# Two attention blocks on one core: V's load on SyncE's queue in a fixed order, and the remainder transposes of steps 4 to 125 by DMA

## The chip, the core and the metric

The kernel runs on one core of a Trainium2 chip. The core has TensorE (PE, which multiplies matrices), VectorE (DVE), ScalarE (ACT), GpSimd (POOL) and SyncE (SP), each with its own stream of instructions. Data moves between the device memory and the on-chip memory by DMA; SP and ACT each issue DMAs into a queue of their own (q1 and q10 in the profile), and 16 DMA engines serve both. The metric is device time in microseconds (us). The kernel before takes 772.24 us, the median of 3 runs (771.94 to 772.95).

## The reference

Two independent problems A and B of the same shape stand side by side in the output. For each, with x of 16x80x576, K and V caches of 16x16x512x128, wq of 576x4096 and wo of 4096x576, all bf16:

```python
q = (x @ wq).reshape(B, Sq, Hq, Dh).transpose(0, 2, 1, 3)      # Hq = 32 heads, Dh = 128
k = jnp.repeat(k_cache, 2, axis=1); v = jnp.repeat(v_cache, 2, axis=1)
scores = jnp.einsum("bhqd,bhkd->bhqk", q, k) * (Dh ** -0.5)
p = softmax(scores, axis=-1)
o = jnp.einsum("bhqk,bhkd->bhqd", p, v)
return o.transpose(0, 2, 1, 3).reshape(B, Sq, Hq * Dh) @ wo
```

Two query heads share one head of K and V, so each K/V head has 160 query rows and 512 keys. The output is 16x80x1152: A's 576 columns, then B's.

## The kernel before, in words

**Steps.** The work is cut into 128 steps (units, U), 64 for each problem. A step is one batch element and four K/V heads. It loads K of the four heads with one transposing DMA (`em_ldk`, L744 to L746, 512 KB) and V with one plain DMA (`em_ldv`, L748 to L750, 512 KB). Each K/V head has 160 query rows and PE's tile has 128, so a step has five score tiles of 128x512: one for the first 128 rows of each head (k = 1 to 4), and one, the **remainder** (k = 0), that holds the last 32 rows of all four heads.

**One score tile.** PE multiplies Q by K into a PSUM bank (`em_qk` L796, the remainder `em_qkr` L782), DVE takes the negated row maximum (`em_max` L805), ACT the exponential with the row sum (`em_exp` L809), DVE the reciprocal (`em_rcp` L815), POOL normalises the tile (`em_nrm` L818). The tile then has to be transposed to pT. By default PE does it with four 128x128 transposes (`em_tr` L824) and DVE copies the result out of PSUM (`em_ptev` L832, the remainder's L830). For the remainders of the steps that `RSEL` (L67) names, SP issues one transposing DMA from p_sb to pT instead (`em_rtr` L836), and there is neither a PE transpose nor a DVE copy. In those steps the remainder also has a reciprocal of its own (`RG`, L66). Then PE multiplies pT by V (`em_pv` L870), 16 matmuls in a step, and ACT takes the result to oT (`em_oev` L886).

**Beside the steps** PE computes Q from x and wq (L672, evicted by ACT L683 or DVE L684) and the output product with wo (L923, evicted at L935, L944 and L951), whose results are stored by SP (L957). Weights come in pieces through SP's queue: wq (L647, L650), wo (L712), and problem B's x by transposing DMAs (L615).

**What sets the order.** A planner inside the kernel's own code (`_Sched`) simulates all engines with assumed durations and writes out, for each engine, a fixed list of instructions; semaphores between them are worked out from that order. Each operation has a stream, a duration, and for the loads a `grid`: a step and an offset from that step's planned time (`tv` plus an offset in us) before which it is not placed. `ahead` lifts its priority above other operations that are ready. Buffers: five slots for K (`NK`), four for V (`NV`), three for pT (`NPT`). K of step U is placed at the time of step U - 6 (`KLEAD`) plus `GK`, V at U - 2 (`VLEAD`) plus `GV`, a remainder's DMA at U - 2 (`RLEAD`) plus `GR_`, a weight piece at its own step (`cycle`, L597 to L606, at most one piece in a step) plus `GW`. A step's scores run 13 tiles (`LA`), 2.6 steps, ahead of its products. From step 10 on K also waits for the PE instruction that the plan has finished just before it (`hard`, L369 to L372). `_Dma.issue` (L120 to L144) is the planner's model of the two queues: when a transfer's data moves, and how long the issuing engine is held. In it a transposing DMA (kind T) of SP and a copy of V (kind V) on ACT's queue wait for each other (`lock`, `copy`).

**Before the change** V of steps 4 to 127 is issued by ACT (`VENG`, L54; 124 loads; the first four are SP's). The remainders of 78 of the 128 steps go by DMA: steps 24 to 45, 70 to 75 and 94 to 125 all, in 18 to 23, 46 to 49, 62 to 69 and 76 to 93 the odd ones, and none before 18 and from 50 to 61.

Of the kernel before, what the change touches and what calls it, by code (L numbers as in the profile page):

```python
# [23 lines left out]
VLAT = 1.05  # L24
VGEN = 2.75
CLAT = 1.3
KLEAD = 6
GK = -1.0
VLEAD = 2
GV = -3.4  # L30
RLEAD = 2
GR_ = 0.95
GW = -3.7
QL0 = 15.0
QL1 = 11.0
KC = 1.85
# [14 lines left out]
NWC = 4  # L51
BANKS = dict(S=(0, 1, 2, 6), T=(3, 4), O=(5, 7), M=(7, 5), M0=(7, 5, 6, 3, 4), M1=(7, 6), ML=(7, 5, 6, 0, 1))
NML = 12
VENG = "act"  # L54
VDUR = 0.42
VU0 = 14
KU0 = 10
XM = dict(wo=6.0, wq=6.0, wqb=6.0, RT=1.5, V=1.5, K=2.0, x=3.0)
# [5 lines left out]
WOC = 1.05  # L64
XDMA = True
RG = (((0, 1, 2, 3, 4),), ((0,), (1, 2, 3, 4)))  # L66
RSEL = ((18, 24, (1, 3)), (24, 46, (0, 1, 2, 3)), (46, 50, (1, 3)), (62, 70, (1, 3)), (70, 76, (0, 1, 2, 3)), (76, 94, (1, 3)), (94, 126, (0, 1, 2, 3)))  # L67
RDC = 0.5
RDK = 2.0
RDO = 10.0  # L70
# [42 lines left out]
class _Dma:  # L113
# [6 lines left out]
    def issue(self, e, st, op):  # L120
        ring = self.ring
        if op.kind == "T":
            d0 = max(st + TLAT, ring["sp"])
            if self.copy[0] < d0 + op.cost and self.copy[1] > d0:
                d0 = self.copy[1]
            end = max(d0 + op.cost, st + op.dur + 0.3)
            self.lock = (d0, end)
            ring["sp"] = end
            return end, max(st + op.dur, end - QRING)
        if op.kind == "V":  # L130
            d0 = max(st + VLAT, ring["act"])
            if self.lock[0] <= d0 < self.lock[1]:
                d0 = self.lock[1]
            end = max(d0 + op.cost, st + VLAT + VGEN)
            self.copy = (d0, end)
            ring["act"] = end
            return end, st + op.dur
        d0 = max(st + CLAT, ring[e])
        c = op.cost
        if e == "sp" and self.copy[0] < d0 + c and self.copy[1] > d0:  # L140
            c += min(c, self.copy[1] - d0)
        end = d0 + c
        ring[e] = end
        return end, max(st + op.dur, end - 6.0)  # L144
# [277 lines left out]
def bass_concat_heads__gqa_block_cached__gqa_block_cached__near_ridge_kernel(  # L422
# [27 lines left out]
    with ExitStack() as es:  # L450
# [21 lines left out]

        sem_names = (["e_pe", "e_act", "e_dve", "e_pool", "d_x00", "d_x01", "d_x10", "d_x11", "d_wo0", "d_wo1",
                      "d_wq0", "d_wq1", "d_wqs", "d_wqt"]
                     + ["d_out%d" % i for i in range(NOSB)]
                     + ["d_r%d" % i for i in range(NPT)]
                     + ["d_k%d" % i for i in range(NK)] + ["d_v%d" % i for i in range(NV)])
# [4 lines left out]
        def R(res, ver):  # L482
            return (res, ver)
# [58 lines left out]
        for half in range(NPP):  # L542
            x_ap = probs[0][0]
            for part, (k0, k1) in enumerate(XP):
                def em_ldx(e, x_ap=x_ap, half=half, k0=k0, k1=k1):
# [5 lines left out]
                      writes=[R(("xs", half * NRT + k_), 0) for k_ in range(k0, k1)], dsem="d_x%d%d" % (half, part),  # L551
# [46 lines left out]
        n = 3  # L598
# [9 lines left out]
        for half in range(NPP):  # L608
            x_ap = probs[1][0]
            st0 = UPR + 16 * half - lead[NG // 2 + 2 * half]  # L610
            for ck in range(5):
                def em_ldxt(e, x_ap=x_ap, half=half, ck=ck):
                    src = x_ap.rearrange("b s d -> (b s) d")[half * NROW:(half + 1) * NROW, :]
                    c0 = ck * 128 if ck < 4 else D - 128
                    return e.dma_start_transpose(xT[:, half, ck:ck + 1, :],  # L615
                                                 src[:, c0:c0 + 128].rearrange("n (c d) -> n c d", c=1))

                S.add("sp", 5.0 * cycle[("x", half, ck)] - 4.0, em_ldxt,
                      writes=[R(("xT", half, b_), 1) for b_ in range(NRT)] if ck == 0 else [R(("xT", half, "t", ck), 1)],
                      dsem="d_x%d0" % half, name="ldxt%d.%d" % (half, ck), stream="x", dur=1.3, cost=0.62, kind="T",  # L620
                      grid=(cycle[("x", half, ck)], GW))

        def qpos(goct, bl):
            return (2 * goct + bl // 4) % NQB * 4 + bl % 4
# [2 lines left out]
        for goct in range(NG):  # L627
# [6 lines left out]
            for pi, (c0, c1) in enumerate(pieces):  # L634
# [9 lines left out]
                for j, (k0, k1, n0, n1) in enumerate(parts):  # L644
                    def em_ldw(e, wq_ap=wq_ap, q=q, wsl=wsl, n0=n0, n1=n1, k0=k0, k1=k1):
                        if k0 == 4:
                            return e.dma_start(wq_sb[64:128, wsl, 4, n0:n1],  # L647
                                               wq_ap[512:576, q * 1024 + n0:q * 1024 + n1])
                        src = wq_ap[k0 * 128:k1 * 128, q * 1024 + n0:q * 1024 + n1]
                        return e.dma_start(wq_sb[:, wsl, k0:k1, n0:n1], src.rearrange("(c p) n -> p c n", p=128))  # L650

                    S.add(eng, t_ld + 0.01 * k0 if goct < 2 else 5.0 * cycle[("wq", goct, j)] - 4.0, em_ldw,
                          writes=[R(("wq", wsl, k0 // 4, p_), wv) for p_ in range(n0 // 256, n1 // 256)], dsem=dsem,
                          name="ldw%d.%d.%d.%d" % (goct, pi, k0, n0), stream=strm if goct < 2 or k0 == 0 else "wqb", dur=0.5,
                          cost=(0.12 + 0.8 * WQC if k0 < 4 else 0.4) * (n1 - n0) / 1024.0 * (1.0 if goct < 2 or k0 else 1.25),
                          grid=(cycle[("wq", goct, j)], GW) if goct > 1 else None)

            for i in range(8):
                for c in range(2):
# [40 lines left out]
        for sg in range(2 * NPAIR):  # L700
# [4 lines left out]
            for n in range(2 * NWC):  # L705
# [4 lines left out]
                def em_ldwo(e, wo_ap=wo_ap, h0=h0, hc=hc, wc=wc, c3=c3):  # L710
# [6 lines left out]
                      writes=[R(("wo", c3, wc), sg)]  # L717
                      + ([R(("warm",), 3 + c3), R(("ones",), 1 + c3)] if sg == 0 and wc == 0 else []),
                      dsem="d_wo%d" % c3, name="ldwo%d.%d.%d" % (sg, c3, wc), stream="wo", dur=0.5, cost=WOC,
                      grid=(cycle[("wo", sg, n)], GW))  # L720

        qk_order = []
        gsize, gfirst = {}, {}
# [313 lines left out]
```

## Time and profile before

| what | value |
|---|---|
| median of 3 runs | 772.24 us (771.94 to 772.95) |
| the profiled execution | 772.67 us |
| its span, first to last instruction | 770.9 us |
| granted PE clock | 1.000 |
| busy: PE, DVE, ACT, POOL | 762.3, 680.0, 607.2, 432.3 us |
| PE matmuls and transposes | 7942, of which 2248 transposes of L824 |
| DMA moved | 170.76 MB, mean 222 GB/s |

The profile comes from one execution. Busy time of an engine is the time in which it executes; the chain that ended last goes back from the last instruction, at each step to what released it. A row of a group gives the source line, engine, operation, output and inputs, how often, then busy time, the mean of one in ns, and the idle time of the engine just before them with what ended it. PE's rows overlap, because matmuls are pipelined. DMA issues are not counted as busy; for them the views give how long the issuing engine was held (least, median and most, in ns) and how long it took from the issue to the landing. In a table of windows the columns are the stretch, its length, the busy time of PE, weight load, DVE, ACT and POOL with their instructions, the granted clock, the DMA engines' busy share, and GB/s.

Issues as the profile has them: K on SP 128 times, held 1302 ns at least and 2748 (A) or 2670 (B) in the median, 5.7 us to landing; remainder on SP 78 times, 1257 ns, 5.3 us; V on ACT 124 times, 375 ns, 5.0 us; V on SP 4 times, 544 ns; wo pieces on SP 32 times, 582 ns; stores on SP 40 times, 366 ns.

### The profile page before, as it was taken

The numbers are of one execution on the slowest core, as the hardware profiler recorded it, in microseconds if no ns is written. First come the engines' busy times: TensorE is split into PE (matmuls) and PEld (weight loads), VectorE is DVE, ScalarE is ACT, GpSimd is POOL, SyncE is SP. The second block draws the span as 40 slices with busy tenths as digits, with TensorE's granted clock in tenths as the row PEclk, the third lists the DMA queues.
The fourth block names the chain that finished last, engine by engine and source line by source line (L and its number), as shares of the span: only waits on it lengthen the run. The fifth ranks groups of instructions, "written<-read, shape, count | busy, mean of one in ns | idle before, by whom it ended". The sixth has DMA issues, their size and how long they took to land.

```text
span 770.9 us, 21081 instructions
## 1 busy us (share of the span) xinstructions
PE 762.3 (99%) x7942; PEld 575.7 (75%) x7942; DVE 680.0 (88%) x1599; ACT 607.2 (79%) x1695; POOL 432.3 (56%) x647
## 2 busy tenths in 40 slices
PE   9899999999999999999999999999999999999998
PEld 5577777777777777777777777777777777777786
DVE  4999999899899999999989989988888988899972
ACT  1888987888888888877778877878888888888860
POOL 1556655655656565655555645654656655565650
PEclk9999999999999999999999999999999999999999
DMA  9999999999999999999999999999999999999931
GB/s 245 235 235 244 217 262 217 228 213 228 206 208 226 248 258 255 239 233 228 205 219 202 220 258 238 249 238 241 220 194 207 198 207 240 241 243 241 248 96 31
DMA packets 422660, 170.76 MB, mean 222 GB/s; under 512 B 319264, under 2 KB 422176, under 8 KB 422560
## 3 DMA queue, kind: packets, MB, share of 16 engines
q1 hardware_dynamic: 355872, 103.22, 74.4%
q10 hardware_dynamic: 66688, 66.20, 29.9%
q8 instruction: 64, 1.05, 0.6%
q14 instruction: 36, 0.29, 0.1%
HBM read 87.46 MB, written 2.95 MB: 117 GB/s over the span
## 4 chain that ended last, share of the span: by engine, by line
PE 94%; DVE 4%; DMA 1%; ACT 1%; issue 0%; SPq 0%
PE ps L672 22%; PE ps L923 20%; PE ps L870 18%; PE ps L824 16%; PE ps L796 13%; PE ps L782 4%; DVE negmax L805 2%; DVE pT L832 1%; DMA acc<-in_A_x_dram 1%; ACT p_sb L809 0%; DVE qT L684 0%; DVE xT L566 0%; DVE pT L830 0%; ACT oT L886 0%; PE ps L562 0%
## 5 line engine op out<-in xcount | busy, mean ns | idle before, releaser
L818 POOL TENSOR_SCALAR p_sb<-p_sb,rinv 128x512 bf16<-128x512 bf16 x640 | 429.9, 692 | 315.6 <-DVE rinv L815 315.4
L809 ACT ACTIVATE p_sb<-ps,negmax 128x512 bf16<-128x512 f32 x640 | 438.8, 691 | 63.8 <-DVE negmax L805 53.9
L805 DVE TENSOR_REDUCE negmax<-ps 128x1 f32<-128x512 f32 x640 | 427.5, 682 | 17.8 <-PE ps L782 9.6
L832 DVE COPY pT<-ps 128x512 bf16<-128x512 bf16 x512 | 210.2, 417 | 15.8 <-PE ps L824 13.3
L870 PE MATMUL ps<-pT,v_sb 128*128 128x160 bf16 x2048 | 219.1, 233 | 0.3 <-issue 0.2
L824 PE MATMUL ps<-ident,p_sb 128*128 128x128 bf16 x2248 | 214.6, 219 | 0.3 <-DVE pT L832 0.2
L672 PE MATMUL ps<-xT,wq_sb 128*128 128x320 bf16 (+2 forms) x1280 | 212.6, 299 | 0.8 <-ACT p_sb L809 0.6
L870 PEld LDWEIGHTS ps<-pT,v_sb 128*128 128x128 bf16 x2048 | 163.3, 98 | 42.5 <-issue 2.0
L796 PE MATMUL ps<-kT,qT 128*128 128x512 bf16 x512 | 193.0, 379 | 1.0 <-ACT p_sb L809 1.0
L824 PEld LDWEIGHTS ps<-ident,p_sb 128*128 128x128 bf16 x2248 | 159.8, 98 | 37.4 <-DVE pT L832 5.9
L923 PE MATMUL ps<-wo_sb,oT 128*128 128x288 bf16 x1280 | 171.3, 286 | 0.1
L672 PEld LDWEIGHTS ps<-xT,wq_sb 128*128 128x128 bf16 x1280 | 116.7, 98 | 54.0 <-ACT oT L886 3.8
L923 PEld LDWEIGHTS ps<-wo_sb,oT 128*128 128x128 bf16 x1280 | 122.7, 98 | 34.2 <-issue 2.1
L886 ACT CAST oT<-ps 128x320 bf16<-128x320 f32 x256 | 108.6, 424 | 44.7 <-PE ps L870 42.0
L809 ACT ACTIVATION_READ_ACCUMULATOR p_sb<-ps,negmax 128x1 f32 x640 | 130.3, 204 | 0.0
L684 DVE TENSOR_SCALAR qT<-ps 128x320 bf16<-128x320 f32 (+2 forms) x138 | 67.4, 488 | 13.4 <-PE ps L672 12.1
L683 ACT ACTIVATE qT<-ps 128x320 bf16<-128x320 f32 (+1 forms) x118 | 51.1, 433 | 31.4 <-PE ps L672 30.9
L796 PEld LDWEIGHTS ps<-kT,qT 128*128 128x128 bf16 x512 | 50.0, 98 | 5.6 <-ACT p_sb L809 2.4
L951 DVE TENSOR_TENSOR osb<-ps,acc 128x288 bf16<-128x288 f32 x40 | 18.3, 457 | 26.9 <-PE ps L923 26.5
L782 PE MATMUL ps<-kT,qT 128*32 128x512 bf16 x512 | 39.6, 384 | 1.9 <-ACT p_sb L809 1.9
L815 DVE RECIPROCAL rinv<-rowsum 128x1 f32<-128x1 f32 (+2 forms) x206 | 34.3, 168 | 6.0 <-ACT p_sb L809 5.7
L830 DVE COPY pT<-ps 128x512 bf16<-128x512 bf16 x50 | 20.8, 416 | 2.3 <-PE ps L824 2.0
(19 smaller groups left out, 47.0 us busy)
## 6 DMA issues: line engine op xcount, KB each, us to landing
v_sb<-in_B_v_cache_dram ACTq DMA_DIRECT2D x64, 512.0 KB, 4.8
v_sb<-in_A_v_cache_dram ACTq DMA_DIRECT2D x60, 512.0 KB, 5.1
wo_sb<-in_A_wo_dram SPq DMA_DIRECT2D x16, 288.0 KB, 5.5
wo_sb<-in_B_wo_dram SPq DMA_DIRECT2D x16, 288.0 KB, 5.0
wq_sb<-in_B_wq_dram SPq DMA_DIRECT2D x16, 256.0 KB, 4.8
out_dram<-osb SPq DMA_DIRECT2D x40, 72.0 KB, 3.3
v_sb<-in_A_v_cache_dram SPq DMA_DIRECT2D x4, 512.0 KB, 5.0
wq_sb<-in_A_wq_dram SPq DMA_DIRECT2D x8, 256.0 KB, 5.1
```

The source lines that it names most:

```text
L672: last = e.matmul(ps[:, vb.phys, 0:n1 - n0], lhsT=wq_sb[:, wsl, ck, i * 128:(i + 1) * 128], rhs=xT[:, half, ck, n0:n1], start=(ck == 0), s ...
L684: return e.tensor_scalar(dst, src, SCALE, None, op0=AluOpType.mult)
L782: last = e.matmul(ps[32 * g4:32 * g4 + 32, vb_.phys, :], lhsT=qT[:, qp_, g4 * 160 + 128:g4 * 160 + 160], rhs=kT[:, ks_, :, g4 * 128:(g4 + ...
L796: return e.matmul(ps[:, vb.phys, :], lhsT=qT[:, qp, gl * 160:gl * 160 + 128], rhs=kT[:, ks, :, gl * 128:(gl + 1) * 128], start=True, stop= ...
L805: return e.tensor_reduce(negmax[:, si:si + 1], ps[:, vb.phys, :], axis=AX.X, op=AluOpType.max, negate=True)
L809: return e.activation(p_sb[:, psl, :], ps[:, vb.phys, :], AF.Exp, bias=negmax[:, si:si + 1], scale=1.0, accum_out=rowsum[:, ss, k:k + 1])
L818: return e.tensor_scalar(p_sb[:, psl, :], p_sb[:, psl, :], rinv[:, ss, k:k + 1], 1.0, op0=AluOpType.mult, op1=AluOpType.mult)
L824: last = e.transpose(psb[:, vt.phys, j * 128:(j + 1) * 128], p_sb[:, psl, j * 128:(j + 1) * 128], ident[:])
L832: return e.tensor_copy(pT[:, pts, :, 0:4, gl * 32:gl * 32 + 32], psb[:, vt.phys, 0:512].rearrange("p (j h c) -> p j h c", j=4, h=4))
L870: last = e.matmul(ps[:, vo.phys, off:off + 160], lhsT=v_sb[:, vs, gl, j * 128:(j + 1) * 128], rhs=pT[:, pts, j, :, gl * 32:gl * 32 + 32], ...
L886: return e.copy(dst, src)
L923: last = e.matmul(ps[:, vb.phys, 0:DC], lhsT=oT[:, hi, rb * 128:(rb + 1) * 128], rhs=wo_sb[:, hi, c3 * DC:(c3 + 1) * DC], start=(hi == 0), ...
```

## The change

V of every step is issued by SP (`VENG`). The offsets of the grid are changed so that the plan issues in each step K (`GK` -2.5), then the weight piece (`GW` -0.6), then V (`GV` -0.55), then the remainder (`GR_` 0.0). `RSEL` names the remainders of all steps from 4 to 125, so 122 go by DMA. The planner's model of a V load follows the queue that issues it, and holds SP back when V's data is planned to end more than 5 us later. Weight pieces and problem B's x get the priority that K and V have (`ahead`), and each wq piece from the third octet on a semaphore of its own.

```diff
-GK = -1.0
+GK = -2.5
 VLEAD = 2
-GV = -3.4
+GV = -0.55
 RLEAD = 2
-GR_ = 0.95
-GW = -3.7
+GR_ = 0.0
+GW = -0.6
...
-VENG = "act"
-VDUR = 0.42
+VENG = "sp"
+VDUR = 0.55
...
-RSEL = ((18, 24, (1, 3)), (24, 46, (0, 1, 2, 3)), (46, 50, (1, 3)), (62, 70, (1, 3)), (70, 76, (0, 1, 2, 3)), (76, 94, (1, 3)), (94, 126, (0, 1, 2, 3)))
+RSEL = ((4, 126, (0, 1, 2, 3)),)
...
         if op.kind == "V":
-            d0 = max(st + VLAT, ring["act"])
+            d0 = max(st + VLAT, ring[e])
             if self.lock[0] <= d0 < self.lock[1]:
                 d0 = self.lock[1]
             end = max(d0 + op.cost, st + VLAT + VGEN)
-            self.copy = (d0, end)
-            ring["act"] = end
-            return end, st + op.dur
+            if e == "act":
+                self.copy = (d0, end)
+            ring[e] = end
+            return end, max(st + op.dur, end - 5.0)
...
+                     + ["d_wq%d_%d" % (i, j) for i in range(2) for j in range(5)]
...
-                      grid=(cycle[("x", half, ck)], GW))
+                      grid=(cycle[("x", half, ck)], GW), ahead=200.0)
...
-                          writes=[R(("wq", wsl, k0 // 4, p_), wv) for p_ in range(n0 // 256, n1 // 256)], dsem=dsem,
+                          writes=[R(("wq", wsl, k0 // 4, p_), wv) for p_ in range(n0 // 256, n1 // 256)],
+                          dsem=dsem if goct < 2 else "%s_%d" % (dsem, j),
...
-                          grid=(cycle[("wq", goct, j)], GW) if goct > 1 else None)
+                          grid=(cycle[("wq", goct, j)], GW) if goct > 1 else None, ahead=200.0 if goct > 1 else 0.0)
...
-                      grid=(cycle[("wo", sg, n)], GW))
+                      grid=(cycle[("wo", sg, n)], GW), ahead=200.0)
```

Since the planner writes out all streams anew, the order of instructions on every engine differs after the change.

## The prediction

> **What bounds the kernel now.** I read the page from the top: busy shares, then the chain that ended last, then the waits of TensorE (PE) and of SyncE, then the DMA queues, then small windows of the trace.
>
> ```profile
> span 770.9 us, 21081 instructions
> ...
> PE 762.3 (99%) x7942; PEld 575.7 (75%) x7942; DVE 680.0 (88%) x1599; ACT 607.2 (79%) x1695; POOL 432.3 (56%) x647
> ...
> PE 94%; DVE 4%; DMA 1%; ACT 1%; issue 0%; SPq 0%
> PE ps L672 22%; PE ps L923 20%; PE ps L870 18%; PE ps L824 16%; PE ps L796 13%; PE ps L782 4%; DVE negmax L805 2%; DVE pT L832 1%; DMA acc<-in_A_x_dram 1%; ACT p_sb L809 0%; DVE qT L684 0%; DVE xT L566 0%; DVE pT L830 0%; ACT oT L886 0%; PE ps L562 0%
> ...
> L824 PE MATMUL ps<-ident,p_sb 128*128 128x128 bf16 x2248 | 214.6, 219 | 0.3 <-DVE pT L832 0.2
> ```
>
> PE is busy for 762.3 of 770.9 us, at a granted clock of 1.00 (the windows further down show it), and 94% of the chain is PE's own work. The rest of the span is mostly the start. The transposes of L824 are 16% of the chain, and PE stood idle 0.3 us before all 2248 of them together. The waits of PE add up to little, and none of them names K, V or a remainder:
>
> ```profile
> engine line waited for: us in total, times, longest us
> PE ps L782 <- ACT p_sb L809: 1.9, 1, 1.9
> PE ps L507 <- DVE wo_sb L500: 1.2, 1, 1.2
> PE ps L796 <- ACT p_sb L809: 1.0, 2, 0.6
> PE ps L672 <- ACT p_sb L809: 0.6, 2, 0.3
> PE ps L562 <- DMA acc<-in_A_x_dram: 0.5, 1, 0.5
> ```
>
> So PE's instruction stream sets the time, and DMA, DVE and ACT matter only if one of them becomes late.
>
> **Price of a transpose on PE.** The mean of 219 ns in the group's row contains a pipeline that overlaps its neighbours: the PE rows of the matmul groups sum to over 1000 us in a span of 771. What a transpose takes from the stream is read from the chain:
>
> ```profile
> by line: PE ps L672 31.7%; PE ps L870 26.6%; PE ps L824 22.3%; PE ps L796 21.6%
> ...
> 640.44 0.22 PE ps L824 x4
> 640.66 0.22 PE ps L796
> ```
>
> That is the chain in 640 to 646 us: four transposes advance it by 0.22 us, 55 ns each. Over the whole chain it is 15.9% of 770.9 us over 2248, or 54.5 ns. I take 55 ns. The Trainium skill (TensorE: Matmul & The Clock Gate, Part 4: PE-mode transpose) gives about 275 ns for one 128x128 bf16 transpose in a kernel; by it the 176 removed here would be worth 48.4 us. The trace disagrees with 55 ns, and the measurement decides.
>
> **The change, part by part.**
>
> *Remainders.* Before, 78 of 128 steps have their remainder transposed by DMA (L836 x78), after it 122. That takes 44 x 4 = 176 transposes off PE: 176 x 55 ns = 9.7 us, all on the path. On DVE go 44 copies of L830 (416 ns each, 18.3 us); 44 more reciprocals come, since a step by DMA normalises its remainder by itself (206 to 250 of 168 ns, 7.4 us). The order of instructions also shows 22 Q evictions passing from DVE (488 ns) to ACT (433 ns): DVE -10.7 us, ACT +9.5 us. DVE ends near 680 - 18.3 + 7.4 - 10.7 = 658 us, further behind PE than now. None of this is on the path except what part of the chain's DVE share goes; L830 shows as 0% there, so under half a per cent, 4 us. I take 0 and keep 4 us for the range.
>
> *V.* 124 loads leave ACT (375 ns of issue each, 46.5 us of its queue) for SP, where an issue took 544 ns in the four V loads that SP already makes: 67 us more for SP. ACT at 607 us was not the bound, so its relief is worth 0; its cover is PE. Of the 128 loads of V 119 carry no wait of their own in the new order, since the wait of the K load ahead covers it; nine wait for PE. So V blocks nobody behind it for long.
>
> *The order of the cycle.* Weight, x and output DMAs keep their number. The 126 cycles carry 72 weight or x pieces (32 of wo, 30 of wq, 10 of x). SP's issues per busiest cycle, from the rows: K 2.7 (median), remainder 1.26, weight 0.58, V 0.54: 5.1 us. PE's unit is (756.3 - 30.4)/128 = 5.67 us between the first and last start of L870, and 9.7/128 less after, 5.59. It fits with 0.5 us over.
>
> *Bytes.* Do K, weight, V and remainder fit one after another on one queue? Three windows in which only one kind moves:
>
> ```profile
> 644.50:645.50 1.00, 1.00 (x11) 0.70 (x9) 1.00 (x4) 0.94 (x3) 0.83 (x2) 1.00 1.08 386
> 647.50:649.00 1.50, 1.50 (x16) 1.23 (x15) 1.50 (x4) 0.75 (x3) 0.00 (x0) 1.00 1.28 291
> 651.60:652.60 1.00, 1.00 (x16) 0.92 (x15) 1.00 (x2) 0.74 (x4) 1.00 (x3) 1.00 1.07 278
> ```
>
> The last number is GB/s: V 386, K 291, mostly wo 278. So K (524 KB) takes 1.80 us, V 1.36, a piece of wo (295 KB) 1.06, a remainder (131 KB, the rate of K) 0.45: 4.67 us in a cycle of 5.59, 84%. That holds on one queue or two. The new bytes are 44 x 131 KB = 5.8 MB, 20 us of a queue that has room.
>
> *How late may a load be?* V is issued two units (11 us) before its use and landed 5.0 us after issue (at most 8.9); the remainder is two units ahead as well and landed after 5.3 (at most 8.4). K is issued six units ahead and used some 3.6 units before the unit's last product (13 steps of lookahead are 2.6 units, a pair's first remainder one more), so 13 us early, with 5.7 to landing and 9.9 at most. Behind V's 1.36 us on the same queue each may land that much later and still be in time. One cost that the trace does not show is what the turn from a transpose to a copy costs on one queue. Nearest below is nothing (the stretch 647 to 653 us passes from remainder to wo to K without a fall in rate); nearest above is the longest that K took to land over its median, 4.2 us, once per cycle. I take nothing, since the same queue already makes that turn with weights; the upper end is the rival below.
>
> *Weights' semaphores.* Ten more, one per piece: PE waits on 32 wq semaphores and not 22, all for pieces loaded cycles before. I cost them at nothing.
>
> **Sum.** The profiled execution took 772.67 us, 1.8 us around the span of 770.9. 772.67 - 9.7 = 763.0. It lies 0.4 us above the median of 772.24, so for a median run 762.5.
>
> **Rivals.**
>
> *SP becomes the bound (slower).* All loads now pass one sequencer, and an issue of K is held while its queue is full. The issues of K in 676 to 716 us (ns, least, median, most):
>
> ```profile
> L746 SPq DMA_TRANSPOSE kT<-in_B_k_cache_dram x7: 2677/3404/4868, 678.9 to 715.7; - x7
> ```
>
> The queues before (q1 is SP's, q10 ACT's: packets, MB, time of the packets as a share of 16 engines):
>
> ```profile
> q1 hardware_dynamic: 355872, 103.22, 74.4%
> q10 hardware_dynamic: 66688, 66.20, 29.9%
> ```
>
> With a median of 3.40 us the cycle is 3.40 + 1.26 + 0.58 + 0.54 = 5.78 us, 0.19 over PE's 5.59; in the 72 cycles with a piece 13.9 us, and 772.2 - 9.7 + 13.9 = 776.4. It decides from a K issue of 3.21 us on, and each 0.1 us more costs 7 us; at the longest of that stretch, 4.87, it would be some 120 us. For it: SP issues without a pause from 682 to 695 us. Against it: there K competes with V on ACT's queue for the same engines, so V's bytes are in 3.40 already; the medians over all K loads, 2.67 and 2.75, leave room; and a passing overrun is taken up by the early issue. The Trainium skill (Perfetto Trace Analysis, DMA Optimizations) holds that with descriptor generation as the limit, balancing DMAs across issuing engines may help, which speaks against this change. The trace agrees only for short stretches. The same skill (DMA: Bandwidth & Descriptors, Issuing engines are not separate DMA queues) holds that a second issuing engine saves issue time alone.
>
> *The gain is eaten.* SP drifts late in the crowded stretches (240 to 300, 640 to 716 us) and PE pays there, by as much as it gained: with 4 to 8 us lost, 766.5 to 770.5; with all lost, 772. The output stores wait in the same queue (L957, over 50 us of waits before), now with V and remainders behind them.
>
> *A transpose is worth its row.* If each removed one freed the 219 ns of its row, it would be 38.5 us and 733.7. The overlap of the rows speaks against it.
>
> *The change does not do what it says.* The order of instructions shows 122 remainders and 128 V loads on SP, so this has no chance.
>
> **Chances.** Forecast, 758 to 766: 0.66. Faster, but partly eaten, 766 to 770.7: 0.11. Eaten, within 0.2% (1.5 us, about what a measurement of this kernel can tell from no change): 0.05. SP the bound: 0.16. A transpose worth its row: 0.02. Faster is then 0.79, same 0.05, slower 0.16. The range 757.5 to 771 holds the forecast's with the 4 us of DVE's share below it, and the partly eaten case: about 0.78.
>
> **What would show it.** Right: L824's successor x2072 with 55 ns a piece in the chain, PE still at 99% with 94% of the chain, DVE near 658 us, no PE wait that names V, K or pT's DMA. SP's issue of K below 3.2 us in the median. Wrong: PE waits for V or K, a gap in PE's tenths in the middle of the span, K's issue over 3.2 us, or V landing later than 11 us after issue. What would make the prediction wrong is above all a turn between copy and transpose on one queue that costs a microsecond or more.

## The result, and the profile after

The changed kernel takes **815.86 us** (median of 4 runs, 810.58 to 821.25) where the kernel before takes 772.60 in the same comparison (771.94 to 773.25): a ratio of 1.056 with a 95% interval of 1.049 to 1.063. It is slower, by more than the rival had said (776.4), and outside the range. The profiled execution took 814.63 us. Ratios here and below leave out every execution that took over 1.5% longer than the fastest one of the same kernel. Line numbers after the change are those of before plus 3 (K's issue is L749, V's L753, the remainder's L839, the store's L960).

From the page of the kernel after (span, busy time, queues with packets, MB and share, the chain by engine and by line, two groups):

```profile
span 812.9 us, 20770 instructions
...
PE 765.0 (94%) x7766; PEld 570.4 (70%) x7766; DVE 664.1 (82%) x1577; ACT 612.5 (75%) x1717; POOL 434.2 (53%) x647
...
PE   8999888999999897999986999889999999998998
...
q1 hardware_dynamic: 445280, 174.01, 105.0%
...
PE 79%; DMA 15%; DVE 3%; ACT 2%; issue 1%; POOL 1%; SPq 1%; DVEq 0%
PE ps L926 19%; PE ps L675 18%; PE ps L873 15%; DMA pT<-p_sb 13%; PE ps L827 12%; PE ps L799 11%; PE ps L785 4%; DVE negmax L808 1%; ACT p_sb L812 1%; DMA out_dram<-osb 1%; DMA acc<-in_A_x_dram 1%; DVE pT L835 1%; POOL p_sb L821 1%; DVE qT L687 0%; PE ps L564 0%
...
L873 PE MATMUL ps<-pT,v_sb 128*128 128x160 bf16 x2048 | 220.0, 233 | 32.1 <-DMA pT<-p_sb 26.9
L827 PE MATMUL ps<-ident,p_sb 128*128 128x128 bf16 x2072 | 197.6, 220 | 2.7 <-DVE pT L835 2.6
```

PE has 176 instructions less and still ends 42 us later. It stands idle for 47.9 us (812.9 - 765.0) where it was 8.6, in dips all over the middle of the span, and one tile has entered the chain that was not in it at all: the remainder's DMA, 13%. PE's waits say the same, and name no wait for K or V (the wait of 6.4 us goes back to an output store that SP issued late, at 436.05 us):

```profile
engine line waited for: us in total, times, longest us
PE ps L873 <- DMA pT<-p_sb: 26.9, 19, 2.8
PE ps L675 <- DVE osb L954: 6.4, 1, 6.4
PE ps L873 <- ACT p_sb L812: 3.2, 2, 2.1
```

The idle time is not all. PE's busy time should have fallen by 9.7 us and rose by 2.7, so its own work took 12.4 us longer than forecast. Most of that is the clock: the granted clock was 1.00 throughout the kernel before, and here it fell to a half in five stretches of 20 us together, in which PE gets through 10 us of work at the full clock. Two of them:

```profile
87.20:90.60 3.40, 3.40 (x20) 2.28 (x19) 2.15 (x5) 2.46 (x7) 2.06 (x4) 0.50 1.15 287
...
438.80:445.60 6.80, 4.94 (x20) 2.93 (x21) 3.73 (x8) 2.23 (x6) 2.70 (x4) 0.50 1.00 247
```

Each of the five begins during a wait of PE of 2.1 to 6.4 us or at most 1.2 us after one; three other waits of 2.2 to 2.8 us were followed by none. So the slower clock goes with the waits. How much of these 10 us adds to the time, and how much would have been waiting anyway, is not shown.

**Why is the remainder late?** SP's timeline (start, length, instruction) shows the queue's order:

```profile
341.05 2.69 SPq L749 DMA_TRANSPOSE kT<-in_A_k_cache_dram  x1
343.79 0.58 SPq L715 DMA_DIRECT2D wo_sb<-in_A_wo_dram  x1
344.41 0.51 SPq L753 DMA_DIRECT2D v_sb<-in_A_v_cache_dram  x1
344.96 1.20 SPq L839 DMA_TRANSPOSE pT<-p_sb  x1
346.20 0.58 SPq L960 DMA_DIRECT2D out_dram<-osb  x1
346.83 2.89 SPq L749 DMA_TRANSPOSE kT<-in_A_k_cache_dram  x1
349.76 0.58 SPq L715 DMA_DIRECT2D wo_sb<-in_A_wo_dram  x1
350.38 0.51 SPq L753 DMA_DIRECT2D v_sb<-in_A_v_cache_dram  x1
351.00 1.70 SPq L839 DMA_TRANSPOSE pT<-p_sb  x1
352.74 3.40 SPq L749 DMA_TRANSPOSE kT<-in_A_k_cache_dram  x1
```

SP issues without a pause, 5.78 us from one K to the next and then 5.91, and PE's unit is 5.59. The queue is the bound, and the last load in its order is the one that PE finds missing.

Is SP really late, or does it wait for others? The view of its waits can't tell, since it puts a wait down to the last update of a semaphore that PE counts up all the time. The counts can: each wait names a count, and the trace has the time of every update. Between 50 and 715 us, PE had released a K load 4.1 us (median) before SP came to it in the kernel after, and POOL a remainder 8.2 us before. In the kernel before, K was released 1.4 us after SP was free, and the remainder 2.6 us before SP came. So SP has turned from an engine that waits for PE into one that PE waits for.

K's issue is what stretches (ns held, least, median and most):

```profile
L749 SPq DMA_TRANSPOSE kT<-in_A_k_cache_dram x64: 2245/3376/7659, 3.3 to 378.3; - x64
L749 SPq DMA_TRANSPOSE kT<-in_B_k_cache_dram x64: 1303/2957/5510, 385.0 to 765.5; - x64
```

Before, the medians were 2748 and 2670. The chain in 391 to 400 us shows how one late remainder stops PE: it went out at 389.08, took 6.02 us, and PE's products start the moment it lands.

```profile
389.08 6.02 DMA pT<-p_sb
395.10 0.09 issue
395.19 0.44 PE ps L873 x4
```

**Where the time is.** From the trace I took the stretches under 8 us between one issue of K on SP and the next (50 to 715 us), grouped by what SP issues in it: W a weight piece, V, R the remainder, S an output store, x a piece of problem B's x. "Idle" is SP's mean idle time in it. "Fetch" means that a transfer of the instruction queue (q8 in the profile, 16 KB each, 64 before and 63 after) begins in it. The table has the largest groups with a remainder.

| kernel, cycle of SP | count | mean us | no fetch / fetch | SP idle |
|---|---|---|---|---|
| before, KR (V on ACT) | 34 | 5.75 | 5.71 / 5.80 | 1.81 |
| before, KRW (V on ACT) | 23 | 5.65 | 5.67 / 5.59 | 0.83 |
| after, KVR | 35 | 5.60 | 5.50 / 5.71 | 0.51 |
| after, KWVR | 41 | 6.07 | 5.57 / 6.60 | 0.26 |
| after, KWVR and S | 12 | 6.81 | 6.18 / 7.45 | 0.28 |
| after, KxVR | 9 | 6.90 | 6.61 / 7.26 | 0.19 |

The last three rows exceed PE's unit of 5.59 by 41 x 0.48 + 12 x 1.22 + 9 x 1.31 = 46 us. The prediction missed by 815.9 - 762.5 = 53. So most of it lies in the cycles with a piece. (Not every microsecond of a store's cycle is new: before the change the nine cycles of K, a piece and a store took 6.01 us, with SP idle for 1.97 of them.) And the plain KWVR cycle without a fetch, 5.57 us, only just equals PE's unit. Whatever comes on top (a fetch 1.03 us in a KWVR cycle, 0.21 in a KVR one; a store 0.74, an x piece in the place of a weight piece 0.83) is lost, where the cycle before had 0.8 to 1.8 us of idle time on SP to take it up.

### The profile page after: what moved, and what is told of

The parts are those of the page before. It is cut to its first block, busy times and chain, and to the rows that moved or that the text cites. A ratio compares the mean times of both kernels' runs of the same rounds, so it can differ in the third digit from the quotient of the medians.

```text
span 812.9 us, 20770 instructions
## 1 busy us (share of the span) xinstructions
PE 765.0 (94%) x7766; PEld 570.4 (70%) x7766; DVE 664.1 (82%) x1577; ACT 612.5 (75%) x1717; POOL 434.2 (53%) x647
## 3 DMA queue, kind: packets, MB, share of 16 engines
q8 instruction: 63, 1.03, 0.6%
## 4 chain that ended last, share of the span: by engine, by line
PE 79%; DMA 15%; DVE 3%; ACT 2%; issue 1%; POOL 1%; SPq 1%; DVEq 0%
PE ps L926 19%; PE ps L675 18%; PE ps L873 15%; DMA pT<-p_sb 13%; PE ps L827 12%; PE ps L799 11%; PE ps L785 4%; DVE negmax L808 1%; ACT p_sb L812 1%; DMA out_dram<-osb 1%; DMA acc<-in_A_x_dram 1%; DVE pT L835 1%; POOL p_sb L821 1%; DVE qT L687 0%; PE ps L564 0%
## 5 line engine op out<-in xcount | busy, mean ns | idle before, releaser
L873 PE MATMUL ps<-pT,v_sb 128*128 128x160 bf16 x2048 | 220.0, 233 | 32.1 <-DMA pT<-p_sb 26.9
L835 DVE COPY pT<-ps 128x512 bf16<-128x512 bf16 x512 | 209.1, 415 | 48.3 <-PE ps L827 45.6
L675 PE MATMUL ps<-xT,wq_sb 128*128 128x320 bf16 (+2 forms) x1280 | 215.6, 302 | 7.0 <-DVE osb L954 6.4
L873 PEld LDWEIGHTS ps<-pT,v_sb 128*128 128x128 bf16 x2048 | 163.0, 98 | 81.4 <-ACT p_sb L812 16.0
L827 PE MATMUL ps<-ident,p_sb 128*128 128x128 bf16 x2072 | 197.6, 220 | 2.7 <-DVE pT L835 2.6
L926 PE MATMUL ps<-wo_sb,oT 128*128 128x288 bf16 x1280 | 173.7, 289 | 0.2 <-ACT oT L889 0.2
L827 PEld LDWEIGHTS ps<-ident,p_sb 128*128 128x128 bf16 x2072 | 148.5, 98 | 35.7 <-issue 5.6
L686 ACT ACTIVATE qT<-ps 128x320 bf16<-128x320 f32 (+1 forms) x140 | 60.9, 435 | 38.9 <-PE ps L675 38.0
L687 DVE TENSOR_SCALAR qT<-ps 128x320 bf16<-128x320 f32 (+2 forms) x116 | 56.7, 489 | 12.6 <-PE ps L675 11.1
L818 DVE RECIPROCAL rinv<-rowsum 128x1 f32<-128x1 f32 (+1 forms) x250 | 40.4, 162 | 11.5 <-ACT p_sb L812 11.2
L938 ACT COPY acc<-ps 128x288 f32<-128x288 f32 x40 | 16.0, 401 | 5.3 <-PE ps L926 4.8
```

The lines of the kernel that those rows point to most:

```text
L675: last = e.matmul(ps[:, vb.phys, 0:n1 - n0], lhsT=wq_sb[:, wsl, ck, i * 128:(i + 1) * 128], rhs=xT[:, half, ck, n0:n1], start=(ck == 0), s ...
L686: return e.activation(dst, src, AF.Identity, scale=SCALE)
L827: last = e.transpose(psb[:, vt.phys, j * 128:(j + 1) * 128], p_sb[:, psl, j * 128:(j + 1) * 128], ident[:])
L835: return e.tensor_copy(pT[:, pts, :, 0:4, gl * 32:gl * 32 + 32], psb[:, vt.phys, 0:512].rearrange("p (j h c) -> p j h c", j=4, h=4))
L873: last = e.matmul(ps[:, vo.phys, off:off + 160], lhsT=v_sb[:, vs, gl, j * 128:(j + 1) * 128], rhs=pT[:, pts, j, :, gl * 32:gl * 32 + 32], ...
L926: last = e.matmul(ps[:, vb.phys, 0:DC], lhsT=oT[:, hi, rb * 128:(rb + 1) * 128], rhs=wo_sb[:, hi, c3 * DC:(c3 + 1) * DC], start=(hi == 0), ...
```

## The experiments

The theories: that one queue can't carry K, piece, V and remainder in PE's unit, whether by its data or by SP's count of issues; that the extra remainders cost it alone; that instruction fetches disturb the transposing DMAs; that the new order of the lists itself costs PE time. Four chips ran them, each with its own runs of the kernel before: one e1 to e4, one e5 and e7 to e9, one e6 and e10 to e14, one e15 and e17. The kernels with DMAs only (e4, e8 to e12) ran once each.

### One part at a time

**e1_rem_alone**, the kernel before with the change's remainders, V still on ACT:

```diff
-RSEL = ((18, 24, (1, 3)), (24, 46, (0, 1, 2, 3)), (46, 50, (1, 3)), (62, 70, (1, 3)), (70, 76, (0, 1, 2, 3)), (76, 94, (1, 3)), (94, 126, (0, 1, 2, 3)))
+RSEL = ((4, 126, (0, 1, 2, 3)),)
```

> The kernel before with one line changed: the remainders of steps 4 to 125 go by DMA, V stays on ACT's queue, the grid stays. Theory 1 (the single queue: on SP's one queue the DMA engines stand still where V's copy gives way to the transpose behind it, and before V's first bytes): two queues fill each other's holes, so 763 to 776 us and little of PE's wait for pT's DMA. Theory 2 (SP's issue time alone: V's 0.54 us per step is what overfills SP): 763 to 768 us. Theory 3 (the 44 added remainder DMAs are the cost, wherever V is): 790 to 815 us.

Measured: 783.14 us in the profiled execution (796.94, 798.08 and 800.88 in the three others) beside 780.62 (774.53 to 785.11) of before. That leaves one run for the comparison, and one gives no interval. Its KRW cycles are 5.32 us without a fetch and 5.88 with one, SP idle 0.27. Even this run is not below the kernel before, so the 9.7 us do not appear with the remainders alone; what they lose on top is not shown. It lies between the ranges of theories 1 and 3.

**e2_v_alone**, the kernel after with before's remainders: the same line the other way round.

> The changed kernel with the remainder selection of before (78 by DMA and not 122), V and the order K, weight, V, remainder on SP. Theory 1: the cycle with all four stays too long where it occurs, so slower than before, 785 to 810 us, and PE waits for pT's DMA or V in steps 24 to 45 and 94 to 125. Theory 2: 44 issues of 1.26 us fewer relieve SP, 775 to 790 us. Theory 3: 772 us, as before.

Measured: 795.05 us, 1.016 (1.009 to 1.023), as theory 1 had it. Its KVW cycles without a remainder are 5.00 us, its KWVR ones 6.66, and the products of L873 wait for the same tile (PE's waits):

```profile
PE ps L873 <- DMA pT<-p_sb: 12.2, 9, 2.8
```

So V's move, in the new order, costs time without one added remainder, in just those cycles that have all four.

**e3_rem_before_v**, the kernel after with the order K, piece, remainder, V:

```diff
-GV = -0.55
+GV = 0.7
-GR_ = 0.0
-GW = -0.6
+GR_ = -0.6
+GW = -1.2
```

> The changed kernel with the remainder issued ahead of V (order K, weight, remainder, V; offsets -2.5, -1.2, -0.6, 0.7). Number of issues and bytes as in the changed kernel. Theory 1, if the turn from V's copy to any transpose costs: it moves to V and the next K, and the time stays at 800 to 820 us, but PE's wait moves from pT's DMA to something else. Theory 1 with a cost that only the remainder after V has: 763 to 775 us. Theory 2: unchanged, 810 to 820 us.

Measured: 850.56 us, 1.088 (1.081 to 1.095), slower than any theory had it. The new order came about in most cycles and not in all: in the trace 34 are K, R, V and 36 K, W, R, V, with a store or without; in 21 with a piece V still goes ahead of R. Moving V behind the remainder is worse, so the place of V between K and the remainder isn't what costs.

**e4_queue_alone**, DMAs only (nothing is computed, the output is zeros). Each stage repeats one cycle 12 times, with four slots to a load, and waits for all to land before the next stage; V behind a "+" is issued by ACT.

```python
STAGES = ("K", "V", "R", "W", "KR", "KV", "KW", "KVR", "KRV", "KWVR", "KWRV", "KVWR", "KR+V", "KWR+V")
...
for i in range(N):
    for j, k in enumerate(main):
        add("sp", k, marks if j == 0 else ())
```

> Only DMAs, no attention: 14 stages of 12 cycles each, with K, V, remainder R (of a constant tile) and a wo piece W of the same shapes, each stage starting when all before has landed: K; V; R; W; KR; KV; KW; KVR; KRV; KWVR; KWRV; KVWR on SP's queue, then KR and KWR on SP with V on ACT's queue. The output is zeros. From the rates of the profile before the sums of data are K 1.8, V 1.36, W 1.06, R 0.45: KVR 3.6, KWVR 4.7 us a cycle. Theory 1: KVR and KWVR exceed these sums by 1 us and more (KWVR 5.8 to 6.8), and with V on ACT's queue the cycle is shorter. Theory 2: KWVR equals the sum of the issue times and has no hole in the data; the cycle with V on ACT is shorter by V's 0.54 us only. The whole is about 600 us long.

Measured, us from one K to the next (or one load to the next), third to last: K 2.60, V 1.52, R 1.31, W 1.10; KR 3.56, KW 3.56, KV 4.54, KVR 5.31, KRV 5.53, **KWVR 5.83**, KVWR 5.70, KWRV 6.48; KR+V 5.55, **KWR+V 5.21**. The windows of the first four stages (K, V, R, W; the last columns are the DMA share and GB/s):

```profile
6.00:31.00 25.00, 0.00 (x0) 0.00 (x0) 1.00 1.12 202
38.00:52.00 14.00, 0.00 (x0) 0.00 (x0) 1.00 1.10 352
58.00:72.00 14.00, 0.00 (x0) 0.00 (x0) 1.00 0.51 103
75.00:86.00 11.00, 0.00 (x0) 0.00 (x0) 1.00 1.00 295
```

Here a term of the prediction falls by itself. It gave K 1.80 us, from a window of 1.5 us that moved 291 GB/s. K after K, with nothing beside it, moves 202 GB/s. The DMA view of 8 to 16 us shows both numbers in one line (40 slices of 0.2 us):

```profile
GB/s 176 155 164 111 56 28 29 234 289 289 289 287 292 268 73 175 148 150 152 152 152 220 97 262 289 287 289 267 273 250 58 55 146 289 284 291 287 291 291 232
```

A transposing load runs at 290 GB/s for a good microsecond and between two of them the rate falls, to 28 to 176. The window had caught a burst. And the remainder, 103 GB/s with the engines half idle, is held by its issue (1.31 us) and not by its bytes (0.45). The stage KV shows what sets K's issue: its first K, with nothing ahead of it, is held for 1.30 us, and those behind a V for 3.5 to 4.8.

### The counts, and the fetches

**e7_v_quarter**, the kernel after with only one head of each V loaded from step 4 on. Three quarters of V's loading are left out; the number of instructions on SP stays.

```diff
-            def em_ldv(e, vc_ap=vc_ap, b=b, q=q, vs=vs):
-                src = vc_ap[b:b + 1, 4 * q:4 * q + 4, :, :].rearrange("b g (p j) d -> p b g (j d)", j=4)
-                return e.dma_start(v_sb[:, vs:vs + 1, :, :], src)
+            def em_ldv(e, vc_ap=vc_ap, b=b, q=q, vs=vs, n=4 if U < NVS else 1):
+                src = vc_ap[b:b + 1, 4 * q:4 * q + n, :, :].rearrange("b g (p j) d -> p b g (j d)", j=4)
+                return e.dma_start(v_sb[:, vs:vs + 1, 0:n, :], src)
```

> The changed kernel, where from step 4 on a V load brings one of the four heads only (128 KB; the other three heads' V stay those of the first four steps, so three quarters of V's loading is left out). Issues, waits and order are as in the changed kernel. Theory 1: the queue's cycle falls by about 1 us below PE's unit and the time to 763 to 772 us, PE-bound, with no wait for pT's DMA. Theory 2: the issues are as many, so 805 to 820 us.

Measured: 761.26 us (760.70 to 762.55) beside 773.87, 0.983 (0.980 to 0.986). Its page, and K's issue:

```profile
PE 751.0 (99%) x7766; PEld 566.9 (75%) x7766; DVE 660.5 (87%) x1577; ACT 610.7 (80%) x1717; POOL 434.3 (57%) x647
...
PE 96%; ACT 1%; DMA 1%; DVE 1%; issue 0%; SPq 0%; DVEq 0%
```

```profile
L749 SPq DMA_TRANSPOSE kT<-in_A_k_cache_dram x64: 1304/2378/7314, 3.3 to 344.5; - x64
```

With the same issues on SP, in the same order, the whole loss is gone. The count of issues alone does not make it. V's bytes do: K's issue falls from 3376 to 2378 ns in the median (problem A), and the KWVR cycle to 5.44 us with 0.63 us idle. The granted clock is 1.00 again.

**e5_no_rem_dma**, the kernel after with `RSEL = ()`: no remainder goes by DMA, V stays on SP.

> The changed kernel with no remainder by DMA: all 128 by PE, V on SP. PE has 312 transposes more than before, 17 us. Theory 1: the cycle K, weight, V has room below PE's 5.8 us, so PE sets the time, 785 to 795 us on a chip where before takes 772, and no wait for V. Theory 2: much the same. Theory 5 (V on SP is the whole fault, remainders none): 815 us or more.

Measured: 787.10 us, 1.016 (1.012 to 1.019), and all of it is PE's own work:

```profile
PE 777.0 (99%) x8254; PEld 593.5 (76%) x8254; DVE 690.1 (88%) x1569; ACT 618.2 (79%) x1725; POOL 434.0 (55%) x647
...
PE 97%; ACT 1%; DMA 1%; DVE 0%; issue 0%; SPq 0%
```

V on SP's queue, the new priorities, the semaphores and the lists cost nothing as long as the remainders stay off the queue (SP is idle 1.73 us in a KWV cycle). With e7 it also gives the price of a transpose where PE is the bound in both: (787.10 - 761.26) / (122 x 4) = 53 ns.

**e8_queue_quiet** and **e9_queue_fetch**, e4 with other stages (v: V of one head, r: a quarter of a remainder), and e9 with 9500 short matmuls on PE, whose code is fetched while the stages run:

```diff
+            for _ in range(NPE):
+                e.matmul(ps[:, 0:128], lhsT=p_sb[:, 0:128], rhs=p_sb[:, 128:256], start=True, stop=True)
```

> Only DMAs, as in e4_queue_alone (output zeros), with the stages KWVR, KWvR, KWVr, KWV, KWR, KWR+V, KW+V, KR+V, KVR of 12 cycles each; v is a V load of one head (128 KB, a quarter), r a remainder of a quarter (32 KB). KWVR and KWR+V repeat 5.8 and 5.0 us a cycle. Theory 1 (the queue's data and its holes): KWvR falls by most of the 1.0 us of data that v leaves out, to 4.9 or less. Theory 2 (SP's issue time): KWvR stays within 0.3 us of KWVR, because the issues are as many, and only KWVr, whose issue is shorter, falls, by 0.8 us or more.

> The same stages (output zeros) with one thing added: PE runs 9500 matmuls of a constant tile beside them, which no DMA waits for, so that PE's instructions have to be fetched (the rows q8 of the profile, 16 KB each, 63 in the changed kernel and none in e4_queue_alone). Theory 4 (each fetch stops the transposes for one to two us): KWVR goes from 5.8 to 6.3 us a cycle or more, KWR+V from 5.0 to 5.4 or more, and low GB/s stand at the fetches' times. If fetches are harmless: every stage within 0.15 us of e8_queue_quiet.

Measured, e8 / e9: KWVR 5.69 / 6.86, KWvR 4.88 / 5.34, KWVr 5.20 / 5.97, KWV 5.26 / 5.65, KWR 4.72 / 4.89, KWR+V 4.91 / 5.70, KW+V 4.61 / 5.06, KR+V 5.83 / 5.69, KVR 5.47 / 4.93 (no fetch fell into this one). The stages that fetches fell into are longer, but PE is busy in e9 and idle in e8, and KR+V and KVR are shorter: not yet a verdict. (The matmuls end at 535 us, within KR+V, so PE is idle in e9's KVR as well: 4.93 and 5.47 are the same stage twice, and show how far one stage scatters between runs.) In e8 the quarter of V takes 0.81 us off KWVR and the quarter of the remainder 0.49, with as many issues: again not the count of issues.

**e10_fetch_none, e11_fetch_few, e12_fetch_many**: 24 cycles to a stage; no matmuls, 3800 of 512 columns, 13000 of 128 columns. PE is busy through the stages in the last two (in e12 until 732 us, early in the last stage), and the number of instructions to fetch differs, with the shape of the matmuls.

> Only DMAs (output zeros), 24 cycles a stage: KWVR, KWR+V, KVR, KR+V, KWR, and KR on SP with V and W on ACT's queue. No stream on PE, so no instruction fetches. KWVR 5.7 and KWR+V 5.0 us a cycle as in both earlier runs; this is the base of the next two.

> The same DMAs (output zeros) beside 3800 long matmuls on PE (512 columns): PE busy throughout, with few instructions, so some 20 to 30 fetches. Theory 4 (the fetches stop the transposes): KWVR within 0.3 us of e10, at most 6.0. If PE's activity, and not the fetch, slows the queue: 6.5 or more, as with the short matmuls.

> The same DMAs (output zeros) beside 13000 short matmuls on PE (128 columns): PE as busy, with some four times the instructions, so about 100 fetches. Theory 4: KWVR 6.5 us or more, about a microsecond added for each fetch that falls into a cycle, and cycles without a fetch as long as in e10. If PE's activity is the cause: the same as e11.

| cycle | e10, no fetch | e11, fetches per cycle | e12, fetches per cycle |
|---|---|---|---|
| KWVR | 5.74 | 5.93, 0.24 | 6.71, 0.90 |
| KWR+V | 4.88 | 5.18, 0.19 | 5.78, 0.81 |
| KVR | 5.46 | 5.45, 0.19 | 5.59, 0.81 |
| KR+V | 5.65 | 5.67, 0.19 | 6.23, 0.86 |
| KWR | 4.58 | 4.70, 0.14 | 4.72, 0.67 |
| KR+VW (both on ACT) | 6.75 | 6.61, 0.24 | 6.67, 0.10 |

A busy PE with few fetches changes KWVR by 0.19 us, one with many by 0.97: (6.71 - 5.74) / 0.90 = 1.08 us for a fetch, on two queues (5.78 - 4.88) / 0.81 = 1.11. That price is not general. In KVR it is (5.59 - 5.46) / 0.81 = 0.16 us and in KWR 0.21, as in the kernel after, where a fetch goes with 1.03 us more in a KWVR cycle and 0.21 in a KVR one. And the expectation that cycles without a fetch are as long as in e10 is borne out in e11 (KWVR 5.70, 16 cycles), but not by the four KWR+V cycles of e12 that have none (6.05). The windows of the KWVR stage, without matmuls (e10) and with many (e12):

```profile
13.60:134.30 120.70, 0.00 (x0) 0.00 (x0) 1.00 1.09 257
```

```profile
12.40:153.30 140.90, 140.90 (x2527) 140.90 (x2525) 0.00 (x0) 0.00 (x0) 1.00 1.18 221
```

The clock is 1.00 in both, and the same loads move at 257 and at 221 GB/s. In the kernel after it looks like this (DMA view of 392.5 to 395.0 us, slices of 62.5 ns; the only fetch of the window begins at 393.0 and takes 1156 ns on one of the engines):

```profile
GB/s 287 242 209 136 90 58 25 16 451 238 258 254 258 270 283 119 53 102 16 12 0 0 0 0 0 0 4 8 8 8 8 12 8 8 8 12 8 12 8 111
...
q8 instruction: 1, 0.02, 2.9%
```

For about 1.3 us, from 393.6 on, nearly nothing moves, while K's load is under way. Such gaps can be counted from the packets (0.6 us or more with under 30 GB/s moved): the KWVR stage has none in e10 and 16 in e12, 14 of them at a fetch; between 50 and 715 us the kernel after has 41, 29 of them at a fetch, and the kernel before 39, 30 of them at a fetch. So the gaps are no news of the change; the time to take them up is gone. Why they come is not shown: that a transposing load must wait for the one engine with the fetch is argued only, and in the stretch above the fetch has ended 0.8 us before the gap does.

**e6_v_act**, the kernel after with V back on ACT (`VENG = "act"`, `VDUR = 0.42`, `GV = -3.4`): the order K, piece, remainder on SP, all 122 remainders.

> The changed kernel with V alone put back on ACT's queue (its issue time 0.42 and offset -3.4 as before); K, weights and remainders stay in the new order, with the new priorities and semaphores, and 122 remainders by DMA. Theory 1 (one queue is the cost): as e1_rem_alone, 1.00 to 1.03 of before, and V's move is then worth the rest up to 1.056. If the new order is the cost and V's place is not: 1.045 or more.

Measured: 780.5 us (774.23 to 785.68) beside 774.62, 1.007 (1.002 to 1.012), as theory 1 had it. Two queues take back most of the loss, with all bytes moved as in the kernel after, but the 9.7 us do not appear. In the profiled execution, of 789.53 us, the KWR cycles are 5.91 us (5.46 without a fetch, 6.52 with one), SP idle 0.22.

The same count of releases orders these kernels. K is released after SP is free by 1.9 us in e5, 1.4 in the kernel before and 0.5 in e7: no time is lost to loads. It is released before SP comes to it by 0.0 us in e1, 0.9 in e6, 2.0 in e2 and 4.1 in the kernel after, and all four lie above the kernel before, the last one farthest. Lateness tells on which side of the bound a kernel lies and not how much it loses: K is released 3.6 us before SP comes to it in e14, 4.2 in e15, and e14 loses more (below).

### Can V's place be chosen by cycle?

From the quiet stages the best choice is V on ACT where the cycle has a piece (4.9 against 5.7 us) and on SP where it has none (5.46 against 5.65, a difference that one stage also shows between two runs). **e13_v_split** does that (72 V on ACT, 56 on SP), **e14_v_split_inverse** the opposite, with the two engines exchanged in `VSEL`. From the diff of e13 to the kernel after:

```diff
+VSEL = lambda piece: "act" if piece else "sp"
...
+        pieces = set(cycle.values())
...
+            von = VSEL(U - VLEAD in pieces)
+            S.add(von if U >= NVS else "sp", 5.0 * U - VK, em_ldv, writes=[R(("V", vs), U)],
...
+                  grid=(U - VLEAD, -0.55 if von == "sp" else -3.4) if U >= VU0 else None,
```

> The changed kernel, with V on ACT's queue (issue time 0.42, offset -3.4) in the steps that also carry a weight or x piece, and on SP as in the changed kernel in the others (72 and 56 loads). 122 remainders by DMA. Theory 1 with 4, by sums: cycles with a piece on two queues 4.9 us and 0.5 fetches of 1.1 us, 5.4; cycles without a piece on one queue 5.5; both below PE's 5.6, so PE sets the time again, 762 to 768 us on a chip where before takes 772 (0.987 to 0.995). If two queues cost by their own collisions whatever the cycle: as e6_v_act, 1.00 to 1.01.

> The inverse: V on SP in the steps with a piece, on ACT's queue in those without. Theory 1 with 4: cycles with a piece 5.7 and 0.55 for fetches, 6.3 us; cycles without one 5.65 to 6.2: as slow as the changed kernel or slower, 1.05 or more of before. If it is the number of V loads on SP that counts (76 here, 128 in the changed kernel): half way, 1.03.

Measured: e13 810.1 us, 1.042 (1.034 to 1.050); e14 825.18, 1.064 (1.056 to 1.071). The direction holds, and e14 came out as expected. But e13 was expected below the kernel before, and is far above it. Its KWR cycles with V on ACT take 5.84 us (5.41 without a fetch, 6.36 with one) and not 4.9, with a store 6.70. SP is behind here too: K is released 2.4 us (median) before SP comes to it, and K's issue is held for 3.55 us. So a cycle measured in repetition doesn't carry over where cycles alternate between queues, and even the fetch-free one is half a microsecond longer in the kernel. Why, these runs do not settle.

### Other traffic off the queue

**e15_store_act** (`STENG = "act"`: the output stores on ACT) and **e17_weights_act** (`WENG = WOENG = "act"`: the weight pieces on ACT, with a semaphore for each piece of wo), each from the kernel after.

> The changed kernel with the 40 output stores issued by ACT and not by SP. In the changed kernel's trace 12 cycles of SP carry K, weight, V, remainder and a store, 6.8 us each where those without the store take 6.1, and SP stands idle 0.3 us in each. If SP's one queue is the bound, taking the store off gives these 0.7 us back, 9 us in all: 1.045 of before. If the stores' place does not matter: 1.055.

> The changed kernel with the 62 weight pieces of steps 2 and later issued by ACT (each with a semaphore of its own), V, K, remainders, x and stores on SP. SP's cycles are then K, V, remainder, 5.6 us in the changed kernel's trace, PE's own unit. If only the length of SP's queue counts: 1.00 to 1.01. If copies on ACT's queue and transposes on SP's hold each other up, as the cycle KR with V and W on ACT's queue, 6.6 us alone, says: 1.03 or more.

Measured: e15 803.73 us, 1.040 (1.037 to 1.042); e17 808.56, 1.045 (1.040 to 1.050). In e15 the cycles with a store fall from 6.81 to 6.33 us, and PE's waits for the remainder stay:

```profile
PE ps L873 <- DMA pT<-p_sb: 23.0, 17, 3.2
```

The stores in SP's queue are worth some 1.6% of the 5.6; the rest is not theirs. In e17 the KVR cycles in which ACT issues a piece take 5.78 us (5.34 without a fetch, 6.39 with one), hardly more than those without a piece (5.72), and less than the 6.07 of KWVR in the kernel after. Yet the time is 1.045 of before, and K is still released 3.2 us before SP comes to it. That the weights collide with the transposes from the other queue, as KR+VW does alone, is not shown by these cycles, and what e17 loses stays open.

No version that does the whole work beats the kernel before.

## Why the prediction was wrong, point by point

**PE bounds the kernel, 55 ns a transpose, 9.7 us: right.** Where SP's queue is relieved (e7) the kernel runs at 99% PE and 12.6 us below before. That is the 9.7 and 2.9 more. The 2.9 fall within the 4 us that were kept for the chain's DVE share, but by luck: e5, with more DVE work than the kernel before (690.1 us against 680.0), lost 13.2 us where 312 transposes at 55 ns are 17.2, so it has such a surplus too. It goes with the new order of the lists rather than with the copies that DVE is spared. The measured price of a transpose is 53 ns. DVE ended at 664.1 us of work (forecast: near 658), far from the path; ACT's relief was worth nothing.

**"It fits with 0.5 us over": this step failed.** 2.7 for K's issue was the median in a queue that had pauses. An issue of K isn't a cost of its own: it is held longer the more lies ahead of it in the queue (e4: 1.30 us with nothing ahead, 3.5 to 4.8 behind a V), so it grows with whatever else is put there, 2.67 to 2.75 before, 2.96 to 3.38 after, 1.99 to 2.38 with a quarter of V. The sum 2.7 + 1.26 + 0.58 + 0.54 = 5.1 took a result of the old queue for a constant. Measured is a KWVR cycle of 6.07 us, with SP idle for 0.26 of it.

**"4.67 us in a cycle of 5.59, 84%. That holds on one queue or two": failed with it, and it is the step that a better reading would have saved.** K's 1.80 us should have been 2.60, the remainder's 0.45 was 1.31 by its issue, V 1.52 and a piece 1.10: 6.53 us one by one, of which the queue overlaps some, and 5.7 to 5.8 are measured. The rate of a window inside a burst was taken for the rate of a stream. The two-queue cycle is 4.9 us, so "one queue or two" was wrong as well. The Trainium skill (DMA: Bandwidth & Descriptors, Issuing engines are not separate DMA queues) holds that a second issuer saves issue time alone; here it saves 5.74 - 4.88 = 0.86 us a cycle in the quiet kernel, and V's issue on SP is 0.51 there.

**"I take nothing" for a turn between copy and transpose.** The value was wrong, and the last section named just this as what would break the forecast. So was the reading that it rests on, that 647 to 653 us pass from the remainder to wo to K without a fall in rate. The DMA view of that stretch of the kernel before (40 slices of 0.15 us) has one, to 34 to 96 GB/s for 0.6 us from 649.25 on:

```profile
GB/s 315 316 279 287 292 295 280 299 285 290 294 287 292 290 156 48 34 48 96 212 328 403 375 389 382 382 374 330 304 280 179 219 309 334 204 303 334 318 236 234
```

But it isn't a matter of the turn from copy to transpose alone: K after K has the same hole, and putting V behind the remainder made things worse (e3).

**The rival "SP becomes the bound" had the mechanism and not the size.** Its cycle of 5.78 us is close to what the quiet queue measures (5.74). It stopped at 776.4 because it counted 0.19 us in 72 cycles. It left out that a queue without idle time also pays for what was free before: the instruction fetches (1.03 us in each KWVR cycle that has one, half of them), the stores that the forecast saw waiting in SP's queue (0.74 more in a KWVR cycle), and the x pieces (0.83 more than a weight piece). Its argument against itself, that an early issue takes up a passing overrun, fails since the overrun never passes.

**Which load is late.** The prediction gave K, V and the remainder room to land later. K and V had it; the remainder, issued last in its cycle and released 8.2 us before SP comes to it, had lost its two units of lead to SP's lateness, as the forecast's own list of signs (a gap in PE's tenths, K's issue over 3.2 us, which holds for problem A's 3.38 and not for B's 2.96) would have it. The list had no sign for PE's clock, which fell with the waits.

**Open.** Why the two-queue cycle takes 5.4 us without a fetch in the kernel and 4.9 alone; why loads stand still for over a microsecond at a fetch of 16 KB, and why that lengthens KWVR and hardly KVR; how much of the time the half clock makes; and KR+V, 5.55 to 5.83 us alone in the mean and thus no better than KVR, though KWR+V gains so clearly (its cycles alternate, in e10 between some 4.8 and some 6.6 us).

## What to carry to other kernels

Before a load is moved to another queue, price the whole cycle of that queue from one issue to the same issue in the next round, and compare it with the unit of the engine that sets the time; a rate read from a window of one transfer, or an issue time from a queue with pauses, understates it. A queue needs slack above its mean cycle, because instruction fetches, stores and rare pieces come on top, and an idle sequencer is where they hid here: whether SP waits for PE's release, or finds it long given, told in these runs which of the two was the bound. A kernel that only issues the DMAs gives the cycle to within a few per cent (5.7 to 5.8 alone, 5.6 without a fetch in the kernel) when one queue carries all, but it did not carry over to cycles split between two.

## What the runs showed of the hardware that had not been expected

- Transposing loads of K, one after the other on an otherwise idle chip, move 202 GB/s on the whole and 290 in bursts; plain loads of V 352.
- A cycle of K, piece, V and remainder with an instruction fetch of 16 KB is longer by 1.03 us in the kernel after, and by 1.08 (one queue) or 1.11 us (two) in the kernels with DMAs only; without the piece it is 0.21 and 0.16. The kernel has some 63 of them.
- The issue of one and the same K load holds SP for 1.30 us with nothing ahead of it in the queue and for 3.5 to 4.8 us behind a V load (e4).
- In the kernel after the granted PE clock fell to a half for 3.4 us four times and for 6.8 us once. In the traces of e1, e2, e3, e6 and e13 to e17 it did so 36 times more, for 3.4 to 10.2 us, and each of the 41 began during a wait of PE of 1.8 us or more, or within 1.5 us after one. The kernel before, e5 and e7 have no wait over 1.9 us, and their clock stayed at 1.00.
- The same loads take 4.9 us a cycle with V on ACT's queue, 5.7 on one, and 6.6 to 6.8 with V and the weights on ACT: the split matters more than the issue times.
